# A planned order over three batches for sliding-window attention and a token mixer, with 64-column transposes in pairs

**Chip, cores, metric.** One core of one Trainium2 chip. The time is device microseconds of one execution, as a median over runs (over the fast ones, where some were slow); lower is better. Every run is put into a state, fast or slow; verdicts compare fast runs with fast runs, at 2%, with a 95% interval.

## The reference

Eight batches, eight heads, 576 tokens, 64 columns a head. The attention sees the token itself and the 127 before it, with a linear distance bias. Its output, as rows of 512 columns, goes through a mixer over tokens.

```python
scores = scale * np.matmul(q, k.transpose(0, 1, 3, 2))          # 8 x 8 x 576 x 576
mask = (rel >= 0) & (rel < 128)
scores = np.where(mask, scores + bias[None], -1000000000.0)
attn = np.exp(scores - scores.max(-1)); attn = attn / (attn.sum(-1) + 1e-09)
x = np.matmul(attn, v) -> rows of 512                           # (arrangement shortened)
wq = x @ w_q;  wk = x @ w_k                                     # 64 columns each
W_tok = scale * np.einsum('bsd,btd->bst', wq, wk)
mixed = np.einsum('bst,btd->bsd', W_tok, x)
out = (np.maximum(mixed, 0.0) @ w_out).astype(np.float32)
```

The kernel never builds `W_tok`: it forms G = wk^T x (64 x 512) and then G^T wq^T, so `mixed` comes out transposed, as the last matmul wants it. The 576 tokens are four tiles of 128 and a tail of 64.

## The kernel before

The order is that of the program text: the attention of batch b, chunk by chunk, with the mixer of batch b-1 in between. Two pools hold PSUM: two score tiles of two banks, each written whole and read whole by one exp, and four tiles of one bank for everything else.

```python
pscore = ... tile_pool(name="pscore", bufs=2, space=PSUM)       # [P, 1024] fp32: two banks each
ppool  = ... tile_pool(name="psmall", bufs=4, space=PSUM)       # one bank each
...
def mk_xpose(tens, st):                                         # q, k: 128 tokens, two heads at a time
    pt = ppool.tile([P, 4, P], F16, name="ptr", tag="p1")
    for c in range(4):
        nc.tensor.transpose(pt[:, c, :n], src, identh[:n, :n])
    cp(eng, dstT[:, :, 128 * st : 128 * st + n], pt[:, :, :n])
...
def mk_mixed(db):
    nc.tensor.matmul(pm, lt, st_["wqT"][:, 0:512], start=True, stop=True)
    nc.scalar.activation(out=rm[:, db, 0:512], in_=pm, func=AF.Relu, scale=WSCALE)   # straight
...
def mk_out(st):
    for db in range(4):
        nc.tensor.matmul(po, rm[:, db, lo : lo + 128], wout_sb[:, db, :], ...)
    cp(nc.vector, osb[pl : pl + n], po[pl : pl + n])
```

## Time and profile before

| | before |
|---|---|
| median of 2 runs | 246.67 us (245.75 to 247.58) |
| span in the profile, granted clock | 246.7 us, 0.85 from 20 to 125 us and 0.80 from 125 to 225 us |
| busy PE / DVE / ACT / POOL | 211.7 / 142.0 / 121.5 / 106.6 us |
| DMA packets | 119,366 |
| first exp, mean time per batch after it, rest after the start of the last batch's first exp | 17.2, 27.2, 38.8 us |

The lines that show PE as the bound, its fall to half clock once a batch and its spacings stand in the prediction. Two more views matter later. The first are two groups of the page (line, engine, operation, out<-in, shapes, count; then busy us and mean ns of one; then idle time before it and who ended that):

```profile
L279 PE MATMUL po<-wout_sb,rm 128*128 128x512 f16 x160 | 50.4, 451 | 0.7 <-ACT rm L268 0.2
...
L268 ACT ACTIVATE rm<-pm 128x512 f16<-128x512 f32 x32 | 19.7, 631 | 0.5 <-PE pml L267 0.5
```

The relu of 128x512 takes 631 ns here; it writes a straight row. The second is the table of waits (engine and line, whom it waited for, us in total, times, longest):

```profile
ACT qT L49 <- PE ptr L130: 80.8, 8, 11.5
...
DVE osb L51 <- PE po L279: 19.2, 26, 6.3
...
DVE invr L182 <- PE px L179: 18.3, 32, 1.2
```

ACT and DVE wait for PE, and each for the matmul whose result it is about to read: the copy to `osb` for the output matmul, the reciprocal for the value matmul. Keep this in mind for the same table after the change.

### The profile page before, as it was taken

What the parts mean: (1) busy time and instruction counts of PE and PEld (TensorE: products, weight loads), DVE (VectorE), ACT (ScalarE), POOL (GpSimd) and SP (SyncE); (2) the same over time, 40 slices, a digit from 0 to 9 for tenths busy, and PEclk for the clock granted to TensorE, in tenths of its full rate; (3) what the DMA queues carried; (4) which work ended last, traced back from release to release, by engine and by line L of the source; (5) the groups of instructions that cost most, each with busy time, mean ns of one, the idle gap of its engine ahead of it and who ended that gap; (6) DMA issues with size and microseconds to landing.
All of it is one profiled execution on the core that took longest, in us unless ns stands there. A gap on an engine that the chain in (4) does not pass through costs nothing.

```text
span 246.7 us, 4766 instructions
## 1 busy us (share of the span) xinstructions
PE 211.7 (86%) x1864; PEld 128.1 (52%) x1864; DVE 142.0 (58%) x362; ACT 121.5 (49%) x218; POOL 106.6 (43%) x132
## 2 busy tenths in 40 slices
PE   0367799889997999889997999889988999889783
PEld 0134576455564656456554656446554656556331
DVE  1124763567645775577556674667656774577413
ACT  2986505880179305970289106950389007930240
POOL 9999938900694019800792039700891000000000
PEclk9999999957996599857995599858995699759979
DMA  3999999972699039962999139922999131003204
GB/s 24 104 141 148 155 112 113 131 50 73 123 166 121 14 117 159 155 39 85 133 163 104 43 90 179 154 20 108 129 161 84 47 125 26 0 0 130 64 24 168
DMA packets 119366, 24.55 MB, mean 100 GB/s; under 512 B 114224, under 2 KB 114736, under 8 KB 119344
## 3 DMA queue, kind: packets, MB, share of 16 engines
q0 software_dynamic: 114096, 14.82, 93.3%
q1 hardware_dynamic: 5248, 9.44, 10.8%
q8 instruction: 14, 0.23, 0.4%
q14 instruction: 8, 0.07, 0.1%
HBM read 29.62 MB, written 9.44 MB: 158 GB/s over the span
## 4 chain that ended last, share of the span: by engine, by line
PE 65%; ACT 13%; DVE 7%; POOL 6%; issue 6%; DMA 2%; ACTq 0%; POOLq 0%
PE po L279 19%; PE px L179 15%; PE ptr L130 7%; PE pxt L198 5%; PE pw L226 4%; PE pk L240 3%; ACT rm L268 2%; DVE osb L51 2%; PE pm L266 2%; DMA vnat<-in_v_dram 2%; ACT qT L49 1%; POOL vnat L113 1%; ACT gm L49 1%; DVE invr L182 1%; PE pg L252 1%
## 5 line engine op out<-in xcount | busy, mean ns | idle before, releaser
L113 POOL DMA_DIRECT2D vnat<-in_v_dram x40 | 34.4, 885 | 77.5 <-issue 59.3
L49 ACT COPY qT<-ptr 128x512 f16<-128x512 f16 (+1 forms) x24 | 12.4, 517 | 80.8 <-PE ptr L130 80.8
L279 PE MATMUL po<-wout_sb,rm 128*128 128x512 f16 x160 | 50.4, 451 | 0.7 <-ACT rm L268 0.2
L143 PEld LDWEIGHTS <-kT 64*128 64x128 f16 x320 | 27.4, 106 | 25.5 <-issue 17.7
L51 DVE COPY osb<-po 128x512 f32<-128x512 f32 (+1 forms) x40 | 27.6, 690 | 19.6 <-PE po L279 19.2
L279 PEld LDWEIGHTS <-rm 128*128 128x128 f16 x160 | 17.1, 116 | 17.3 <-issue 10.1
L182 DVE RECIPROCAL invr<-px 128x4 f32<-128x4 f32 (+1 forms) x80 | 13.3, 175 | 19.8 <-PE px L179 18.3
L51 DVE COPY kT<-ptr 128x512 f16<-128x512 f16 (+1 forms) x24 | 9.1, 381 | 20.0 <-PE ptr L130 18.8
L268 ACT ACTIVATE rm<-pm 128x512 f16<-128x512 f32 x32 | 19.7, 631 | 0.5 <-PE pml L267 0.5
L266 PE MATMUL pm<-wqT,gm 64*128 64x512 f16 x32 | 14.1, 474 | 5.8 <-ACT gm L49 0.7
L51 DVE COPY xT<-pxt 128x512 f16<-128x512 f16 (+1 forms) x40 | 15.5, 388 | 1.0 <-PE pxt L198 0.5
L49 ACT CAST wqT<-pw 64x512 f16<-64x512 f32 x8 | 4.6, 579 | 16.8 <-PE pwl L228 16.8
L49 ACT COPY kT<-ptr 128x512 f16<-128x512 f16 x16 | 9.4, 586 | 5.8 <-PE ptr L130 5.8
L226 PE MATMUL pw<-xT,wqk_sb 128*64 128x512 f16 x32 | 10.1, 416 | 0.0
L51 DVE COPY qT<-ptr 128x512 f16<-128x512 f16 x16 | 6.7, 421 | 3.0 <-PE ptr L130 2.3
L269 ACT ACTIVATE rm<-pml 128x64 f16<-128x64 f32 x32 | 8.5, 264 | 0.0
L51 DVE CAST wkn<-pk 128x256 f16<-128x256 f32 (+1 forms) x16 | 4.4, 315 | 5.6 <-PE pk L240 5.6
L252 PEld LDWEIGHTS <-wkn 128*64 128x64 f16 (+1 forms) x40 | 3.7, 108 | 7.4 <-issue 3.3
L266 PEld LDWEIGHTS <-gm 64*128 64x128 f16 x32 | 3.0, 95 | 8.0 <-ACT gm L49 1.0
L240 PE MATMUL pk<-wqk_sb,xT 128*128 128x64 f16 (+1 forms) x160 | 7.1, 195 | 0.0
L267 PE MATMUL pml<-wqT,gm 64*128 64x64 f16 x32 | 6.7, 208 | 0.0
L240 PEld LDWEIGHTS <-xT 128*128 128x128 f16 (+1 forms) x160 | 5.8, 100 | 1.5 <-issue 0.2
(752 smaller groups left out, 562.0 us busy)
## 6 DMA issues: line engine op xcount, KB each, us to landing
out_dram<-osb SPq DMA_DIRECT2D x32, 256.0 KB, 2.0
vnat<-in_v_dram POOLq DMA_DIRECT2D x32, 128.0 KB, 5.0
out_dram<-osb SPq DMA_DIRECT2D x8, 128.0 KB, 4.0
vnat<-in_v_dram POOLq DMA_DIRECT2D x8, 64.0 KB, 4.7
wout_sb<-in_moe_w_out_dram POOLq DMA_DIRECT2D x1, 512.0 KB, 6.2
qnat_107<-in_q_dram POOLq DMA_DIRECT2D x1, 128.0 KB, 3.5
knat_109<-in_k_dram POOLq DMA_DIRECT2D x1, 128.0 KB, 3.4
qnat_111<-in_q_dram POOLq DMA_DIRECT2D x1, 128.0 KB, 3.4
```

Of the source, the lines that this page charges most:

```text
L49: eng.copy(out_ap, in_ap)
L51: eng.tensor_copy(out=out_ap, in_=in_ap)
L113: nc.gpsimd.dma_start(out=vnat[:n, kt, 0:H, 1:65], in_=v[b, :, ss, :].transpose([1, 0, 2]))
L130: nc.tensor.transpose(pt[:, c, :n], src, identh[:n, :n])
L143: nc.tensor.matmul(pss[i][:, o : o + w], kT[hb : hb + 64, hp, 128 * kb : 128 * kb + 128], qT[hb : hb + 64, hp, 128 * kb : 128 * kb + w], s ...
L179: nc.tensor.matmul(px[:, hh, :], lt, rt, start=(i == 0), stop=(i == len(mms) - 1))
L182: nc.vector.reciprocal(out=invr[:n], in_=px[:n, :, 0])
L226: nc.tensor.matmul(pw[0:64], wqk_sb[:, dc, 0:64], xT[:, dc, 0:512], start=(dc == 0), stop=(dc == 3))
L240: nc.tensor.matmul(pk[:n, t, :], xT[:, dc, 128 * t : 128 * t + n], wqk_sb[:, dc, 64:128], start=(dc == 0), stop=(dc == 3))
L266: nc.tensor.matmul(pm, lt, st_["wqT"][:, 0:512], start=True, stop=True)
L268: nc.scalar.activation(out=rm[:, db, 0:512], in_=pm, func=AF.Relu, scale=WSCALE)
L279: nc.tensor.matmul(po, rm[:, db, lo : lo + 128], wout_sb[:, db, :], start=(db == 0), stop=(db == 3))
```

## The change

The intent: less TensorE work, fewer DMA descriptors, and no more turns between exp and matmuls. A planner inside the kernel simulates five engines with assumed lengths, lets work of three batches compete, gives every intermediate a PSUM bank, and emits the instructions in the order found. The core of the diff (cut; some 750 lines are new):

```diff
-pscore = ... bufs=2 ([P, 1024]);  ppool = ... bufs=4 (one bank)
+pair = [ppool.tile([P, 2, 512], FP32, name=f"bank{i}", tag=f"bank{i}") for i in range(4)]
+def bank(key):                       # slot 0..7 chosen by the planner
+    s = pl.slot[key]
+    return pair[s // 2][:, s % 2, :]
+def wide(key):                       # scores: both banks
+    return pair[pl.slot[key] // 2]
...
+# q, k: rows of four tokens, one load of q and one of k per batch
+nc.gpsimd.dma_start(out=dst[i][:, h0:h1, :], in_=blocks(src, b, h0, h1))
...
+# transposes of 64 columns, two side by side
+for i in range(2):
+    nc.tensor.transpose(pb[64 * i:64 * i + 64, a, :, j, :],
+                        src[i4][:, h, 64 * j:64 * j + 64], identh)
...
+# q stays in the order (token mod 4, token div 4); the relu puts the order right
+relu(e, rm[i2][:, 2 * hf + i, :].rearrange("p (t g j) -> p t j g", t=4, j=4),
+     bank(keys[hf]).rearrange("p (t j g) -> p t j g", t=4, j=4))
...
+# tails of two batches in one 128-row tile; scores of two heads always together;
+# one projection for wq and wk; G and the mixing in pairs
...
+order = pl.run()
+for o in order:
+    o.fn(o.eng)
```

The relu is given to ACT or DVE, and the planner assumes 0.49 us (ACT) or 0.60 us (DVE) for it. The planner's own estimate of the whole is 161.4 us.

> **What bounds the kernel now.** I read the page first (span, busy table, slices, chain), then the table by stretches over one batch in the middle, then the timelines of single engines to get the spacing of back-to-back instructions; the waits came last and only confirm.
>
> ```profile
> span 246.7 us, 4766 instructions
> PE 211.7 (86%) x1864; PEld 128.1 (52%) x1864; DVE 142.0 (58%) x362; ACT 121.5 (49%) x218; POOL 106.6 (43%) x132
> ...
> PE   0367799889997999889997999889988999889783
> ...
> ACT  2986505880179305970289106950389007930240
> ...
> PEclk9999999957996599857995599858995699759979
> ...
> PE 65%; ACT 13%; DVE 7%; POOL 6%; issue 6%; DMA 2%; ACTq 0%; POOLq 0%
> ```
>
> TensorE is busy 86% of the span and makes up 65% of the chain that ended last, so it sets the time, helped by a chain through exp (ACT 13%). ACT comes in bursts (9, then 0), and in every batch the granted TensorE clock falls to half just behind such a burst. Cutting out one batch shows it (columns: busy time of PE, PEld, DVE, ACT, POOL; then clock, DMA share, GB/s):
>
> ```profile
> 98.69:126.01 27.32, 25.30 (x233) 15.46 (x233) 17.61 (x46) 14.00 (x27) 12.57 (x16) 0.81 1.16 110
> 103.60:113.40 9.80, 8.79 (x69) 5.26 (x67) 6.49 (x19) 5.86 (x12) 0.31 (x1) 0.50 0.71 45
> 113.40:126.01 12.61, 12.21 (x138) 7.79 (x136) 8.25 (x24) 3.23 (x8) 7.35 (x9) 0.99 1.02 144
> ```
>
> The chain repeats every 27.32 us. In 9.80 us of that the clock is 0.50, so the 8.79 us PE is busy there hold work of about half that: 4.4 us a batch are lost to the clock, 2.0 us to idle PE, and 27.3 - 4.4 - 2.0 = 20.9 us is work at full clock. Seven such periods are 191 us; the rest is the first batch (the first exp starts at 17.23) and the last batch's mixer (from about 229 to 246.7).
>
> The third view is the timeline of PE (start, length), where starts give the true spacing, since the lengths contain the pipe:
>
> ```profile
> 114.11 0.22 PE L179 MATMUL px<-vnat,pt_1399 128*128 128x65 f16 x2
> 114.17 0.22 PE L179 MATMUL px<-vnat,pt_1402 128*128 128x65 f16 x2
> ...
> 116.17 0.34 PE L179 MATMUL px<-vnat,pt_1402 128*128 128x65 f16 x2
> 116.44 0.34 PE L179 MATMUL px<-vnat,pt_1425 128*128 128x65 f16 x2
> ...
> 120.35 0.39 PE L130 MATMUL ptr<-identh,qnat_1680 128*128 128x128 f16 x4
> 120.57 0.39 PE L130 MATMUL ptr<-identh,knat_1682 128*128 128x128 f16 x4
> ...
> 125.47 0.28 PE L143 MATMUL ps_1_1808<-qT,kT 64*128 64x256 f16 x1
> 125.47 0.28 PE L143 MATMUL ps_0_1807<-qT,kT 64*128 64x256 f16 x1
> 125.58 0.27 PE L143 MATMUL ps_1_1808<-qT,kT 64*128 64x256 f16 x1
> ...
> 127.36 0.61 PE L143 MATMUL ps_0_1833<-qT,kT 64*128 64x256 f16 x5
> 127.97 0.57 PE L143 MATMUL ps_1_1834<-qT,kT 64*128 64x256 f16 x4
> ```
>
> To be seen: a value matmul pair (x2) costs 0.06 us, 30 ns each, but 0.27 us a pair in the last query tile, where a 64-row and a 128-row matmul alternate: about 0.1 us for each change. A 128x128 transpose costs 55 ns (four in 0.22). Two heads' score matmuls that meet run together (two of 256 columns in 0.11 us), but mostly the heads go one behind the other, 0.60 us each.
>
> **What the Trainium skill says.** "TensorE: Matmul & The Clock Gate", Part 1 (The HAM clock gate), says that the array runs at 1.2 GHz unless recently busy and at 2.4 GHz after a busy window of about 3.4 us. The trace agrees: 1.00 or 0.50 and nothing between, half clock behind the stretch where PE waited for exp. "TensorEngine Tiling (Array Packing)", Key Properties, says tiles work in parallel and that changing the tiling mode drains the engine; the trace shows both for rows (0.11 us for two, 0.1 us a change). For column tiles, which the new transposes use, no run here shows it yet. "Advanced Engine Details and Errata", Clock Domains, has 42 to 43 ns for an unobstructed 1 KiB DMA descriptor; before has no such loads. "Perfetto Trace Analysis", What "DMA-bound" means, counts the issuing sequencer as a DMA bound of its own: here POOL takes 885 ns for the 1024 rows of a vnat issue, 13.8 ns per row and DMA engine.
>
> **The change part by part**, TensorE per batch of 27.32 us, full-clock spacings from above.
> - q, k transposes: now 32 at 55 ns plus 8 half ones, 2.1 us. New: 64 transposes of 64 columns in side-by-side pairs. 32 pairs at 55 ns if they fully overlap, 110 if not; I take 80 (64-column weights may load more slowly): 2.6 us. The tail tokens of several batches share tiles, 128 half transposes in all: 64 pairs at 60 ns over 8 batches, 0.5. Sum 3.1, a loss of 1.0.
> - Scores: now 8 heads at 0.60 = 4.8. New: always two heads at once, 1024 columns at 0.11 per 256 = 0.44, with small ones 0.48; four times, 1.9. Gain 2.9.
> - Values: now 64 at 30 ns + 8 pairs at 0.27 = 4.1. New: 72 at 30 ns = 2.2, because the last tile uses all 128 rows (zeroed v rows). Gain 1.9.
> - x transposes: 20 become 18 at 55 ns, 1.0, no change.
> - Mixer projections: now 4 x 0.25 (pw and pwl) + 0.8 (pk) = 1.8. New: one projection for both, 18 matmuls of 128 columns at 55 ns = 1.0, plus 9 half transposes, 0.4. Gain 0.4.
> - G: 5 x 0.22 = 1.1 becomes 5 column pairs of 256 columns, 0.6. Mixing: 4 x 0.25 = 1.0 becomes row pairs, 0.5. Gain 1.0.
> - Output: 5 x 0.86 = 4.3 becomes 4.5 x 0.86 = 3.9. Gain 0.4.
>
> New sum 3.1 + 1.9 + 2.2 + 1.0 + 1.4 + 0.6 + 0.5 + 3.9 = 14.6. To it come mode changes: per batch 4 transpose groups, 4 score groups, 5 or so small ones; 13 groups with two changes each, less those that lie side by side, some 16 at 0.1 us, 1.6. So TensorE needs 16.2 us a batch at full clock, against 20.9. The larger part of the gain is that the planned order interleaves three batches, so that exp and matmuls no longer take turns and neither the 4.4 us of half clock nor the 2.0 us of idleness should stay.
>
> ACT and DVE: exp every 0.92 us x 8 = 7.4 (ACT only); bias products every 0.60 x 8 = 4.8 and ten normalisations at 0.44 = 4.4 (DVE only). PSUM copies, given to whichever is free: q, k 3.0 (k's are permuted, so I give them 0.9 on ACT), xT 1.2, projections and G 1.1, relu 2.0, outputs 4.5 x 0.5 = 2.2, tails 1.2. Total 27.3, 13.7 each if split evenly: 84% of 16.2. Close, but second.
>
> DMA: before issues 1024 rows per 128 tokens at POOL's pace, 13 full and partial issues and two more a batch, POOL busy 12.57. New: q and k one issue each, five of v, small tails: about 7.3 us of POOL. Data per DMA engine: 144 rows of 1 KiB x 42 ns = 6.0, 288 v rows x 13.8 = 4.0, stores about 2.9 (estimate: 10.8% of 246.7 over 8 gives 3.3, less the overhead of one issue): 12.9 of 16.2. Hidden, with three input buffers.
>
> Start and end: the first exp at about 10 instead of 17.23, because q and k come in head pairs first and the iota comes behind them. At the end the last two batches' mixers follow each other; their outputs are dense PE work and counted, but the dependent steps in front (projection, copy, G, copy, mixing, relu) leave PE idle some 5 us, and closing takes 3.3 us as now (last copy ends 243.4 of 246.7).
>
> Sum: a fixed order on five engines loses something to waits the plan did not foresee; I take 5%, so 17.0 a batch. 10 + 8 x 17.0 + 8 = **154 us**, ratio 0.62.
>
> **The rivals.**
> 1. Column pairs don't overlap. Then transposes cost 110 ns a pair (+1.2 with tails) and G 1.1 (+0.5): 17.9 a batch, with 5% 18.8, 168 us. For it: no column pair runs in the trace of before. Against: row pairs do overlap, and the page speaks of both alike.
> 2. ACT and DVE become the bound. 13.7 needs a perfect split and copies at the prices above; permuted copies at a slower pace, or waits of in-order queues at 80% use, make it 13.7/0.8 = 17.1, the same 155 us, or 18.5 and 166 us if the copies land 10% dearer. For it: three engines near the same load in a fixed order; against: DVE and ACT are idle over 40% of the time now.
> 3. The order misses: an engine waits in line for the wrong thing, PE falls to half clock again for part of each batch. With 3 us lost a batch, 178 us. Against it: work of three batches is at hand.
> 4. Everything fits: pairs at 55 ns, few mode changes, no stalls, 14.8 a batch: 136 us.
> 5. DMA binds: 42 ns would have to grow to 65 under load to pass 16.2; then loads would arrive late in every batch.
>
> **Range and chances.** Rival 4 gives 136, rivals 1 and 2 166 to 168; weighing, 8 in 10 lie in **141 to 171**. To be not faster by 2% it would have to lose 88 us against the sum, so faster by over 2% 0.97, within 2% 0.02, slower 0.01.
>
> **What would show it.** PEclk near 1.0 after about 12 us, without a dip per batch, mean over 0.93 (else rival 3). PE busy over 85% between 20 and 135 us; starts of a new ptr pair 80 ns apart (rival 1: 110 or more). Score groups of two heads in about 0.48 us. ACT and DVE both at 75 to 85% of the span; if either is at 95% in the middle and PE waits for it, rival 2. POOL near 60 us in all, DMA packets near 60,000, and no PE wait on a DMA after the first batch. First exp before 11 us. The prediction is wrong in its core if PE is busy under 75% in the middle, or if the period per batch is outside 15 to 19 us.

## The result, and the profile after

After: 268.02 us (266.4 to 269.65), in the fast state, correct. Ratio to before 1.0867 [1.0683, 1.1051]: **slower**. Ratios here are the mean time of one kernel's fast runs over that of the other's of the same rounds, so not quite the ratio of the medians quoted. The page of after:

```profile
span 267.9 us, 5355 instructions
...
PE 175.0 (65%) x2248; PEld 115.9 (43%) x2248; DVE 154.4 (58%) x344; ACT 132.8 (50%) x167; POOL 63.6 (24%) x89
...
PE   0566667676649479678766686667575865548471
...
PEclk9996558959895957997979569999886699655589
```

```profile
PE 37%; DVE 33%; ACT 17%; issue 7%; DMA 2%; POOL 2%; ACTq 0%; DVEq 0%; POOLq 0%
```

PE's busy time did fall, from 211.7 to 175.0 us. But of 40 slices only two show a 9 for PE (before has 20), and DVE and ACT are below 60%. The chain that ended last was 65% PE before; now PE has 37% of it, DVE 33% and ACT 17%. No engine is the bound: they wait for each other. The table of stretches (length; busy time of PE, PEld, DVE, ACT, POOL; clock, DMA share, GB/s) says that it is so from end to end, with the last stretch worst:

```profile
44.00:98.00 54.00, 36.05 (x494) 24.57 (x491) 35.15 (x74) 31.21 (x35) 13.59 (x16) 0.80 1.21 115
98.00:153.00 55.00, 39.78 (x567) 27.35 (x566) 37.54 (x83) 31.13 (x39) 13.60 (x16) 0.84 0.81 106
153.00:208.00 55.00, 38.62 (x540) 25.40 (x538) 35.99 (x78) 31.24 (x39) 1.55 (x2) 0.87 0.22 50
208.00:268.00 60.00, 35.12 (x265) 17.33 (x263) 18.24 (x40) 18.84 (x27) 0.00 (x0) 0.73 0.18 62
```

The table of waits says what is odd about it:

```profile
ACT osb L368 <- PE bank L736: 31.8, 16, 3.7
...
DVE rm L695 <- ACT osb L368: 17.7, 4, 10.4
...
DVE invr L528 <- ACT osb L368: 15.0, 7, 5.8
...
ACT kT L368 <- DVE qT L370: 7.5, 1, 7.5
```

A reciprocal needs the sums of a value matmul. Here it waits for ACT copying a finished output tile, which no step of the reference connects with it. The timeline, a few us in which the three engines take turns, shows how (start, length, engine, line; in brackets the idle time before it and what ended that):

```profile
99.78 0.58 ACT L368 COPY osb<-bank 128x512 f32<-128x512 f32 x1 [2.00 <-PE bank L736]
...
100.42 0.60 PE L520 MATMUL bank<-vn,pt 128*128 128x65 f16 x8 [0.72 <-ACT osb L368]
...
101.05 0.58 ACT L368 COPY osb<-bank 128x512 f32<-128x512 f32 x1 [0.69 <-PE bank L520]
...
101.67 0.18 DVE L528 RECIPROCAL invr<-bank 128x4 f32<-128x4 f32 x1 [5.75 <-ACT osb L368]
101.88 0.42 DVE L529 TENSOR_TENSOR xs<-bank,invr 128x256 f16<-128x256 f32 x1
...
103.24 0.58 ACT L368 COPY osb<-bank 128x512 f32<-128x512 f32 x1 [1.61 <-PE bank L520]
...
103.86 0.18 DVE L528 RECIPROCAL invr<-bank 128x4 f32<-128x4 f32 x1 [1.55 <-ACT osb L368]
```

PE's value matmul waits for an output copy, the next output copy for that value matmul, the reciprocal for that copy. I looked up such waits in the built program, where each instruction names its tile and bytes: one reciprocal that waits for an ACT copy reads bytes 2304 to 3088 of tile `bank3`, and the copy reads bytes 0 to 2048 of it. Nothing overlaps; they only share the tile, that is, they lie in its two banks. So the framework that puts in the waits tracks whole tiles. The program of after has 808 waits on an engine's counter (694 of them on another engine's); 207 are on an instruction that touches only the other bank of the tile. (Such counts are of the built programs, not of a trace.) Before has no such pairs, because its shared work lies in one-bank tiles and a score tile is always used whole.

The second odd group is the relu, 1300 ns on both engines where before has 631:

```profile
L695 DVE TENSOR_SCALAR rm<-bank 128x512 f16<-128x512 f32 x17 | 21.5, 1300 | 27.8 <-ACT osb L368 17.7 <-PE bank L714 8.2 <-PE bank L520 1.9
L693 ACT ACTIVATE rm<-bank 128x512 f16<-128x512 f32 x15 | 19.2, 1317 | 6.2 <-DVE xs L529 2.8 <-DVE qT L370 2.3 <-PE bank L714 1.1
```

Theories. **A:** the waits on the other bank of a two-bank tile stretch the planned order. **B:** the dearer relu, 1.30 us where the planner has 0.49 or 0.60, does it. **C**, a rival to the size of A: the order is bad because it was planned with wrong lengths, whatever the tiles. **D**, for what stays: input data that land later than their place in the order.

That two engines need to be held apart inside one bank is no mistake. The Trainium skill, "PSUM — Partial Sum Buffer", section "PSUM bank collisions raise a hardware error", says that two engines may not touch the same bank and 32-partition quadrant at once, reads against reads included, that different banks run clean, and gives the rule to guard by bank and quadrant. So even the wait of one reader for another (ACT `kT` for DVE `qT` above) is right inside a bank; after guards by pairs of banks. No run here tried to let two engines into one bank at once; all the split versions below that keep the arithmetic are correct.

### The profile page after: what moved, and what is told of

Its sections match the earlier page's. It is cut to its first block, busy times and chain, and to the rows that moved or that the text cites. A ratio compares the mean times of both kernels' runs of the same rounds, so it can differ in the third digit from the quotient of the medians.

```text
span 267.9 us, 5355 instructions
## 1 busy us (share of the span) xinstructions
PE 175.0 (65%) x2248; PEld 115.9 (43%) x2248; DVE 154.4 (58%) x344; ACT 132.8 (50%) x167; POOL 63.6 (24%) x89
## 2 busy tenths in 40 slices
DMA packets 63400, 24.59 MB, mean 92 GB/s; under 512 B 39824, under 2 KB 58768, under 8 KB 63376
## 4 chain that ended last, share of the span: by engine, by line
PE 37%; DVE 33%; ACT 17%; issue 7%; DMA 2%; POOL 2%; ACTq 0%; DVEq 0%; POOLq 0%
PE bank L736 14%; DVE rm L695 7%; DVE xs L529 6%; ACT osb L368 6%; PE bank L438 5%; DVE pt L492 5%; PE bank L520 4%; ACT rm L693 3%; DVE invr L528 3%; PE bank L714 3%; DVE xT L370 2%; PE bank L473 2%; DVE qT L370 2%; DVE kT L370 2%; DMA kn<-in_k_dram 2%
## 5 line engine op out<-in xcount | busy, mean ns | idle before, releaser
L487 ACT ACTIVATE pt<-bank 128x1024 f16<-128x1024 f32 x64 | 62.7, 1034 | 17.2 <-PE bank L473 16.2
L287 POOL DMA_DIRECT2D vn<-in_v_dram x40 | 33.7, 849 | 83.9 <-PE bank L520 76.2
L736 PE MATMUL bank<-wout_sb,rm 128*128 128x512 f16 x128 | 46.5, 518 | 9.4 <-ACT osb L368 3.5
L520 PE MATMUL bank<-vn,pt 128*128 128x65 f16 x576 | 31.5, 209 | 19.9 <-DVE rm L695 5.5
L492 DVE TENSOR_TENSOR pt<-pt,btab 128x1024 f16<-128x1024 f16 x64 | 42.7, 684 | 1.8 <-ACT pt L487 1.6
L520 PEld LDWEIGHTS <-pt 128*128 128x128 f16 x576 | 26.4, 108 | 28.7 <-issue 24.3
L695 DVE TENSOR_SCALAR rm<-bank 128x512 f16<-128x512 f32 x17 | 21.5, 1300 | 27.8 <-ACT osb L368 17.7
L528 DVE RECIPROCAL invr<-bank 128x4 f32<-128x4 f32 (+1 forms) x80 | 14.2, 177 | 30.7 <-ACT osb L368 15.0
L529 DVE TENSOR_TENSOR xs<-bank,invr 128x256 f16<-128x256 f32 x64 | 27.1, 424 | 2.3
L473 PE MATMUL bank<-qT,kT 64*128 64x256 f16 (+1 forms) x256 | 25.0, 300 | 4.9 <-ACT pt L487 3.1
L438 PE MATMUL bank<-identh,qn 128*64 128x128 f16 x256 | 13.4, 260 | 16.5 <-DMA qn<-in_q_dram 6.6
L693 ACT ACTIVATE rm<-bank 128x512 f16<-128x512 f32 x15 | 19.2, 1317 | 6.2 <-DVE xs L529 2.8
L473 PEld LDWEIGHTS <-kT 64*128 64x128 f16 x320 | 13.4, 106 | 10.6 <-issue 5.1
```

The costliest lines, as they stand in the source:

```text
L287: nc.gpsimd.dma_start(out=vn[i][0:n, kt, :, 0:D], in_=v[b, :, 128 * kt:128 * kt + n, :].transpose([1, 0, 2]))
L438: nc.tensor.transpose(pb[64 * i:64 * i + 64, a, :, j, :], src[i4][:, h, 64 * j:64 * j + 64], identh)
L473: nc.tensor.matmul(ps[i][:, o:o + w], lt[hb:hb + 64], rt[hb:hb + 64], start=True, stop=True)
L487: nc.scalar.activation(out=pt_t[pl.slot[pk]], in_=wide(key).rearrange("p a c -> p (a c)"), func=AF.Exp, scale=SCALE)
L492: nc.vector.tensor_tensor(out=pt, in0=pt, in1=btab[h], op=ALU.mult)
L520: nc.tensor.matmul(px[:, hh, :], pt[:, o:o + 128], vn[i4][:, kt, h, :], start=(n == 0), stop=(n == len(mms) - 1))
```

## The experiments

All ran beside before, on the chip of their job (e1 to e4 on one chip, e5, e6 and e8 on a second, e9b and e10 on a third, e11 on a fourth; before's median was 246.4 to 248.11 us in these jobs). Where a kernel had slow runs, the fast ones alone are compared. Kernels marked "wrong on purpose" leave the output in a wrong order or read wrong rows; their instructions and shapes are otherwise those of the kernel they stand for.

### Part of the tiles split, nothing else: e1_split3

```diff
-pair = [... for i in range(4)]
+pair = [... for i in range(3)]
+one = {i: ppool.tile([P, 512], FP32, name=f"one{i}", tag=f"one{i}") for i in (6, 7)}
 def bank(key):
     s = pl.slot[key]
-    return pair[s // 2][:, s % 2, :]
+    return one[s] if s in one else pair[s // 2][:, s % 2, :]
```

> The planned order and every instruction stay as they are; only the PSUM tile of two banks that carries most of the small results (banks 6 and 7) is split into two tiles of one bank. The built program waits on a sibling bank at 207 places before and at 85 after. Theory A (false waits: an engine waits for work in the other bank of a two-bank tile) expects 225 to 250 us from 268. Theory B (the relu copies of 1.3 us against a planned 0.5 set the loss) expects no change, 262 to 270. Theory C (a fixed order with wrong durations stalls whatever the tiles are) expects no change too.

Measured: 223.03 us (221.92 to 225.14), ratio 0.9034 [0.8971, 0.9097], correct, 2 us under theory A's range. In the built program the instructions that touch data are the same as in after, on each engine in the same order; waits on the other bank fall from 207 to 85. So 45 us go with waits alone, from one tile of four. The first q and k of the run show it singly. After (the slot of q is one bank of a tile, that of k the other):

```profile
7.26 0.64 PE L438 MATMUL bank<-identh,qn 128*64 128x128 f16 x8 [1.78 <-DMA qn<-in_q_dram]
...
7.68 1.07 PE L438 MATMUL bank<-identh,kn 128*64 128x128 f16 x16
...
8.79 0.69 DVE L370 COPY qT<-bank 128x1024 f16<-128x1024 f16 x1 [1.12 <-PE bank L438]
...
9.52 1.01 ACT L368 COPY kT<-bank 128x1024 f16<-128x1024 f16 x1 [7.50 <-DVE qT L370]
...
10.58 0.64 PE L438 MATMUL bank<-identh,qn 128*64 128x128 f16 x8 [1.83 <-ACT kT L368]
```

The same in e1_split3:

```profile
6.35 0.64 PE L439 MATMUL one<-identh,qn 128*64 128x128 f16 x8 [0.86 <-DMA qn<-in_q_dram]
...
6.78 1.06 PE L439 MATMUL one<-identh,kn 128*64 128x128 f16 x16
...
7.59 0.63 DVE L371 COPY qT<-one 128x1024 f16<-128x1024 f16 x1
...
7.88 1.01 ACT L369 COPY kT<-one 128x1024 f16<-128x1024 f16 x1 [5.87 <-PE one L439]
...
8.76 0.64 PE L439 MATMUL one<-identh,qn 128*64 128x128 f16 x8 [0.91 <-DMA qn<-in_q_dram]
```

In after, the copy of q starts only once k's transposes into the other bank have ended, k's copy once q's copy has ended, and the next transposes once k's copy has ended: three waits in a row. In e1 each copy starts when it needs to; they overlap, and PE waits for data alone.

### All small tiles of one bank: e2_splitall

```diff
-one = {... for i in (6, 7)}            # on top of e1
+one = {... for i in (4, 5, 6, 7)}
-for p in (0, 1, 2):                    # pairs that scores may take
+for p in (0, 1):
```

> Banks 4 to 7 are four tiles of one bank, scores use the two pairs left; the order is planned anew with that (the plan's own estimate goes from 161.4 to 159.5 us, so the order is no better or worse by plan). Sibling-bank waits 7 in place of 207. Theory A expects 185 to 215 us; theory B and C 255 to 272.

Measured: 194.08 us over the three fast runs (191.86 to 194.28; the slow one took 195.61), ratio 0.7825 [0.7763, 0.7888], correct; 7 waits on another bank are left. Its profiled run fell in the slow state, so I read no clock from it. Here the planner made a new order, since scores have two pairs and not three; its own estimate moves from 161.4 to 159.5 us, by 2 of the 74 us gained. So 45 of the 74 us are shown with the order held fixed (e1); for the other 29 the split and the new order are not taken apart.

### The relu written straight, tiles as in after: e3_flatrelu (wrong on purpose)

```diff
-relu(e, rm[...].rearrange("p (t g j) -> p t j g", t=4, j=4), bank(keys[hf]).rearrange(...))
+relu(e, rm[i2][:, 2 * hf + i, :], bank(keys[hf]))
```

> Wrong rows in the output on purpose: relu writes its result in the order in which it reads it, in place of a stride of four elements; the two-bank tiles stay. Relu should fall from 1.30 us to about 0.6, 36 full ones, so some 13 us off each of ACT and DVE. Theory B expects 225 us or less (half of the 107 us between the plan's 161 and 268 and more); theory A expects only what the relus on the chain are worth, 10% of the span in the chain of waits shortened by half: 250 to 260. Theory C 250 to 262.

Measured: 243.65 us in the only fast run, at clock 0.878; the other three were slow (247.73 to 248.07, clock 0.84), so the record gives no ratio and no verdict. That is some 24 us under after (20 with the slow runs): B is real, but not of the size that it expected (225 or less), and on its own it brings the kernel only near the time of before. The relus are down to 690 ns on DVE and 599 on ACT, and those on DVE still wait most for ACT's copies to `osb`:

```profile
L695 DVE TENSOR_SCALAR rm<-bank 128x512 f16<-128x512 f32 x17 | 11.5, 690 | 23.3 <-ACT osb L368 15.4
```

### Both: e4_split_flat (wrong on purpose)

The edits of e2_splitall and e3_flatrelu together.

> Both: single-bank tiles and the flat relu (wrong rows on purpose). If A and B together are the cause: 165 to 190 us, near the plan's 159.5 plus some stalls. If a third cause is large (theory C: order, half clock, loads): over 200.

Measured: 183.6 us (182.98 to 185.49), ratio 0.7441 [0.739, 0.7492]. So the split is worth 74 us with the dear relu and some 60 us with the cheap one (243.65 - 183.6, from one fast run of e3); the relu is worth some 24 us in two-bank tiles and 10.5 in single ones (194.08 - 183.6). That fits a long read that holds up the other bank as well, but I did not test it by itself.

### Both, and correct: e5_split_natq

q is put into token order when it is copied out of PSUM, as k already was; then the relu has nothing to put right.

```diff
 o = dst[i2][:, 2 * half:2 * half + 2, :]
-if ti == 0:
-    copy(e, o, bank16(key).rearrange("p (a c) -> p a c", a=2))
-else:
-    copy(e, o.rearrange("p a (b g j) -> p (a b) g j", b=4, j=4),
-         bank16(key).rearrange("p (c j g) -> p c g j", c=8, j=4))
+copy(e, o.rearrange("p a (b g j) -> p (a b) g j", b=4, j=4),       # for q as for k
+     bank16(key).rearrange("p (c j g) -> p c g j", c=8, j=4))
...
-nc.gpsimd.iota(wint[:, 0:256], pattern=[[128, 2], [1, 4], [4, 32]], ...)
+nc.gpsimd.iota(wint[:, 0:256], pattern=[[1, 256]], ...)
```

> Correct results: single-bank tiles, and q is put into token order when it is copied out of PSUM (as k already is), so relu reads and writes straight and the stride of four is gone from 36 relus. Theories A and B together expect what the wrong-on-purpose version with both gave, 183.6 us, plus up to 16 q copies that are 0.5 us longer on DVE: 183 to 192. If the strided relu was cheap to begin with, 192 to 196.

Measured: 185.86 us (185.72 to 186.02), ratio 0.7502 [0.7465, 0.7538], fast, correct: faster than before by 25%. Moving the permutation to the read of q's copy costs DVE 1.22 in place of 0.69 us for 128x1024, ACT nothing (1.02 either way). The groups, to be held against those of after:

```profile
L691 DVE TENSOR_SCALAR rm<-one 128x512 f16<-128x512 f32 x19 | 12.5, 684 | 8.5 <-PE one L710 7.8 <-ACT gm L369 0.7
...
L689 ACT ACTIVATE rm<-one 128x512 f16<-128x512 f32 x13 | 7.7, 600 | 0.2 <-PE one L710 0.2
```

The relu again waits mostly for its own matmul. The stretches of e5, the last begun when the first exp of batch 7 was some 5 us away:

```profile
65.00:131.00 66.00, 56.99 (x928) 39.64 (x922) 53.14 (x129) 54.55 (x74) 16.08 (x20) 1.00 1.20 156
131.00:184.00 53.00, 41.85 (x536) 26.27 (x530) 33.88 (x86) 31.15 (x48) 0.00 (x0) 0.99 0.26 91
```

PE is busy 86% (56.99 of 66) at full clock, ACT 83% and DVE 81%. The chain that ended last, from start to end of the run, is no longer mainly PE's:

```profile
DVE 36%; PE 27%; DMA 15%; POOL 12%; issue 4%; ACT 3%; DVEq 0%; ACTq 0%; POOLq 0%
```

### The lengths in the plan: e6_split_durs

e2_splitall with the measured relu told to the planner (`ev(512)` becomes 1.25 and 1.23 us; the tail's 0.68 and 0.66).

> Single-bank tiles with the strided relu as it was; only the plan is told its true length (1.25 in place of 0.5 us), so the order changes. Theory C (the order suffers because the plan has wrong lengths) expects clearly under the 194.2 us of the same tiles without this, 180 to 189. Theory B (the work itself costs) expects 190 to 197. The plan's own estimate rises from 159.5 to 169.5.

Measured: 194.8 us over the two fast runs (194.75 and 194.9; the slow ones took 199.24 and 200.11), ratio 0.7861 [0.7812, 0.7911], no better than e2's 194.08. C falls as far as the relu's length goes: a plan with the true relu gains nothing. Other lengths in the plan were not corrected; when loads land is taken up below.

### More banks per tile: e8_quad

```diff
-pair = [... for i in range(4)]
+pair = [... for i in range(2)]
+quad = ppool.tile([P, 4, 512], FP32, name="bank4to7", tag="bank4to7")
+pair += [quad[:, 0:2, :], quad[:, 2:4, :]]
```

> The other way round: banks 4 to 7 become one tile of four banks, same order and instructions as the changed kernel. Waits on another bank of the same tile 415 in place of 207. Theory A expects about as much loss again as the two-bank tiles cost, 300 to 360 us from 268. The rivals, in which the tiles don't matter, 262 to 272.

Measured: 424.53 us (422.47 to 425.7), ratio 1.7121 [1.7036, 1.7207], correct, clock 0.659 in the profiled run; well above the 300 to 360 us that A expected. Again the data instructions are those of after in the same order; 415 of 824 waits are on another bank. (A recount by a slightly different rule gives 85, 216 and 423 in e1, after and e8.) With order and work of the program fixed, 85, 207 and 415 such waits give 223, 268 and 425 us. What differs besides names is waits and signals. That is A; its direction was foreseen, its size was not, and the time does not grow in proportion to the count.

### Is the rest input data? e9b_vcoarse (wrong on purpose), e10_tails, e11_tails_late

e4 and e5 still lie over 20 us above the planner's 159.5 and 161.7. Set against the plan, their exps start 3 to 4 us late at the first and 13 us late at the fourth batch, 17 to 18 us late in the last: most of the lag arises early. There PE stands for q (table of waits of e4):

```profile
PE one L439 <- DMA qn<-in_q_dram: 11.2, 5, 4.7
```

e9b is e4 with v in rows of four tokens, to wrong places, which takes all packets from 63,400 to 34,984. (A first build, e9_vcoarse, was refused because it gave values that are not finite; it never ran. In e9b the second step of the normalisation is a comparison, 425 ns as the product is in e4.)

```diff
-in_=v[b, :, 128 * kt:128 * kt + n, :].transpose([1, 0, 2])
+in_=blocks(v, b, 2 * kt, 2 * kt + 2)       # wrong places, a quarter of the descriptors
```

> Wrong result on purpose. Single-bank tiles and straight relu as in e4_split_flat (183.6 us), and v loaded in rows of four tokens, to wrong places: the packets of v fall to a quarter, the order of all engines stays. If the some 20 us that e4 still lies above its plan come from input transfers that arrive late in the first batches (DMA share above 1.8 of 2 there, waits of PE for qn): 172 to 178 us, and the lag of exp against the plan at the fourth batch falls from 13 us to under 8. If they come from elsewhere (dependent steps that are longer than planned): 181 to 185 us and the lag stays near 13.

Measured: 179.84 us (179.07 to 181.34), ratio 0.7273 [0.7226, 0.732]; lag at the fourth batch 8.9 us. It falls between the two answers I had written: transfers are worth about 4 us of the end (183.6 - 179.84) and 4 us of the early lag, not all of it.

e10 is e5 with the loads of the tails of batches 2 to 7 moved back (`-39.0 + 12 * n` becomes `-39.0 + 25 * n` in the planner's due time), so that batch 1 goes ahead.

> Correct. e5_split_natq (185.86 us) with one number changed: the tail loads of the batches 2 to 7 are issued about half a batch later, so that they no longer stand ahead of the second batch's q, k and v in the DMA queues. If early transfers are what the rest of the loss is made of, PE's wait for qn in the second batch shrinks by some 4 us and the time is 180 to 183 us. If not: 185 to 187.

Measured: 183.81 us (182.5 to 184.63), ratio 0.7428 [0.7371, 0.7486], correct: the lowest correct time, 2 us under e5, with intervals that overlap. The lag at the second batch stayed at 5.5 us and at the fourth it was 13.4. The wait moved:

```profile
40.61 1.06 PE L402 MATMUL one<-identh,qnt 128*64 128x128 f16 x16 [4.45 <-DMA qnt<-in_q_dram]
```

e11 adds a later due time for the transposes of these tails (`14.0 + half` becomes `24.0 + half`).

> Correct. e10_tails (183.81 us) with a second number changed: the transposes of those late tails stand some 10 us later in the order, because in e10 PE stood 4.45 us at 36 to 41 us for the tail loads that had been moved back. If the early loss is input data that arrives after its place in the order: 178 to 182 us, no such wait, and the lag of exp against the plan at the fourth batch is under 10 us (e10: 13.4). If the lag only moves to another load: 183 to 185 us.

Measured: 185.04 us (183.37 to 185.57), ratio 0.7491 [0.7429, 0.7552]. The edit missed its aim: the plan puts the first of these transposes at 30.7 us with either number, because it believes that the loads have landed by then; on the chip PE stood 5.25 us for them, until 40.45 us. So e11 doesn't decide between its two answers. What e10 and e11 show of D is that the plan takes transfers to land earlier than they do, and that moving one load moves the wait to another. The lag at the fourth batch was 14.7 us in e11, no better than before the edit.

## Why the prediction was wrong

The prediction said 154 us (141 to 171) and gave "slower" one chance in a hundred; after takes 268.02 and is slower. Point by point:

- **The step that failed** is "a fixed order on five engines loses something to waits the plan did not foresee; I take 5%": 0.8 us a batch. The measured period is 23.4 us against 17.0 (first exp at 19.5, first exp of batch 7 at 183.6, seven periods between), and the rest after it 84.3 us against 25. The waits were in the diff: `pair` is declared with two banks, and I read it as eight banks. e1 and e8, with the order fixed, show them as cause, and e2 agrees. With single-bank tiles and the straight relu (e5) the period is 17.04 us. Of the 82 us between after and e5, 74 go with the split and its new order (e2) and the other 8 with the relu, less what q's permuted copy costs.
- **Rival 3** named the right symptom, an engine waiting in line for the wrong thing and PE at half clock, at 3 us a batch and 178 us. It was given too little: its reason against, that work of three batches is at hand, doesn't help where a finished result can't be read because of its neighbour. The clock of 0.802 has no cause of its own: PE's instructions are the same in e1, where it is 0.895, and in e8, where it is 0.659.
- **A term mis-sized:** "relu 2.0" a batch. By the groups shown it is (21.5 + 19.2)/8 = 5.1 us without the tails, because the write has a stride of four elements: with a straight write and nothing else changed (e3) one takes 599 and 690 ns. I priced permuted reads of k, not permuted writes.
- **Start:** the first exp came at 19.5 us, not 10. The split brings it to 18.1 (e1) and 17.1 (e5); the rest, in e5, is q and k arriving in pieces, so that their transposes last from 4.6 to 12.1 us, and the tail transposes from 13.2 to 16.6 that stand before the first scores at 16.5.
- **A term hidden by the large one:** "10 + 8 x 17.0 + 8" closes too early. In e5 the parts are 17.1 + 7 x 17.04 + 47.5 = 183.9: the end is 22.5 us longer than 17 + 8. That is not idleness: in the last 53 us PE is busy 79%. An order that interleaves three batches leaves mixers of earlier batches behind the last batch's exps; the plan itself has 42.8 us there (118.9 to 161.7). For the same reason it is luck that the period of e5, 17.04 us, is the predicted 17.0: between the first exps of batch 0 and batch 7 PE is busy 95.95 of 119.29 us, which is 13.7 us a batch and not 16.2, and idle 3.3 us and not 0.8. So even with A and B away the kernel lies above my range.
- **What held:** column pairs do overlap (rival 1 falls). At full clock, in after as in e5, the two of a pair start within 4 ns of each other and the next pair 56 ns later, or the two alternate some 28 ns apart; either way a pair costs 56 ns: the rate of rival 4, better than the 80 ns I took. In a score group of e5 (its 256-column matmuls and their small ones) all starts lie within 0.40 us and the next instruction starts 0.45 us after the first at the earliest, against 0.48. POOL 63.6 us against near 60; 63,400 packets against near 60,000. In e5 PE is busy 86% from 65 to 131 us, but 82% from 20 to 135 us, where over 85% was named; ACT and DVE have 70 and 75% of the span against 75 to 85%.
- **Rivals 2 and 5** came true in part once the false waits were gone. In the middle of e5 PE, ACT and DVE are at 86, 83 and 81%, so no engine has much to spare. The DMA share is 1.98 from 30 to 60 us, where before has 1.28 from 20 to 125 us, and PE waits on a DMA in later batches too (2.92 us for q, until 44.65 us), which "no PE wait on a DMA after the first batch" denied. (The forecast's 6.0 us of DMA for q and k is an estimate from the skill's 42 ns a row; no view here times one such row.) Rival 2's sum has a slip: with the copies, 10.7 of the 27.3 us, 10% dearer, 80% use gives 17.7 us and 160, not 18.5 and 166.
- **What stays open:** of the 23 to 24 us by which e4, e5 and e10 exceed their plans, 3 to 4 lie before the first exp and about 4 go with v's descriptors. The rest isn't separated.

## What to carry to other kernels

Look at how buffers are declared before counting on overlap: a tile is the unit in which a tracking framework waits, so independent work that shares a tile is not independent, and a planner that hands out banks must hand out tiles of one bank. In the table of waits, look for a pair that the algorithm doesn't connect; that is the mark of a false dependency, and splitting the tile, with nothing else changed, is the test. And when work is spread over several batches, add the fill and the drain as work of their own, not as one period each.

## What the Trainium skill lacked or had wrong

- "PSUM — Partial Sum Buffer" gives the rule to guard by bank and quadrant, but not what a coarser guard costs. Here the same instructions in the same order took 223, 268 and 425 us with 85, 207 and 415 waits on a neighbouring bank.
- "SBUF — State Buffer", section "Door 1: The DMA port swizzle", counts 8 bf16 elements, 16 bytes, as how far one can stride for free. An fp16 write of 128x512 with a stride of 4 elements (8 bytes) was not free: 1317 in place of 599 ns on ACT, 1300 in place of 690 on DVE (after against e3).
- No page says whether ScalarE pays for a permuted fp16 read out of PSUM. Here it did not: 1.02 us for 128x1024 either way.
- "TensorEngine Tiling (Array Packing)" has no spacing for back-to-back transposes in pairs of column tiles, nor has another page: a pair of 64 columns started every 56 ns here at full clock, as one full 128x128 transpose does (55 ns).
